# A hand-ordered attention-and-MLP kernel: decay scan and weight decoding as single steps, a new order for all queues, and one pool of PSUM banks

## Chip, core and metric

The kernel runs on one core of a Trainium2 chip. The metric is the device time of one execution in microseconds (us). TensorE (PE) does the matmuls, its weight loads are the row PEld; VectorE is DVE, ScalarE is ACT, GpSimd is POOL, and SP's queue issues the DMA loads and stores.

## What is computed

A gated linear attention, followed by an MLP with a hardswish. The first runs over 4 batches of 8 heads, 768 tokens and 48 columns a head; the second takes its output as 3072 tokens of 384 columns.

```python
for t in range(S):                       # S = 768, for each of 4 x 8 heads
    state = alpha[t][:, None] * state + outer(k[t], v[t])
    y[t] = q[t] @ state
x = y.transpose(0, 2, 1, 3).reshape(3072, 384)
h = x @ w_in                             # 384 x 2048
g = h * clip(h + 3, 0, 6) / 6
out = g @ w_out                          # 2048 x 384
```

The weights come in float64 and are passed as pairs of 32-bit words, so the kernel decodes them itself.

## The kernel before

**Attention.** The 3072 tokens are cut into 24 chunks of 128 (`j` = 0 to 23, six a batch). Per chunk: the decay is scanned backwards over the chunk (`r`, a scan on VectorE, and the reciprocal of its first column), then forwards from that reciprocal (`p`). `k` and `q` are multiplied with the two scans (steps `k`, `q`), scores are formed on TensorE (`sc`) and masked on VectorE (`m`); `qa`, `sv` are ScalarE copies that put q and the state beside the scores and v; `kb`, `ck` turn k by token (for later chunks `kt`, `kw`, `kr` do that by a VectorE transpose and a trip through DRAM); `u` and `sm` update the state, `st` (POOL) decays it; `ya`, `yb` form the output and `cy` copies it out. For the first six chunks alpha, k and q are transposed on TensorE (`ta`, `tk`, `tq`) and alpha is copied by ScalarE (`ca`); from chunk 6 on VectorE transposes them. `la`, `lk`, `lq`, `lv` load alpha, k, q, v.

**Weights.** 16 slices of 768 KB: 0 to 7 are `w_in`, 8 to 15 `w_out`. `w` loads a slice into a staging buffer (five at first, three from slice 5 on). `d1` and `d2` (ScalarE, `dx` for slices 0, 1, 2, 4), `d3` (VectorE, two instructions for these four slices, three for the others), and `d4` (POOL) decode it. A staging buffer is loaded again only after `d4`.

**MLP.** Two chunks form a group. Groups 0 and 1 take the plain first layer: `f` (or by halves `fa`, `fb`), `fr` on ScalarE and `fg` on VectorE make the hidden values. Group 0 takes the plain second layer `b`. From group 2 on the first layer is a scheme of sums and 20 products in which fewer products are needed: `xc` sums the inputs (VectorE), `M` is a product (TensorE, line 600), `n` copies a partial bank to SBUF (ScalarE, line 606) before the next product goes on in the same bank, `o` combines (VectorE), `e` and `h` gate. `y` sums the weights once. From group 1 on the second layer does the same with 7 products `P` (line 703), sums `s`, copies `K`, outputs `G` (VectorE, or ScalarE for the fourth) and stores `O`; `x` sums its weights. `z` are matmuls of the identity that feed nothing.

**What sets the order.** Every step is a word, `name.numbers`; one list of 1788 words is walked under a manual schedule, and each engine's queue holds its instructions in the order of the list. An engine waits for the first instruction of its queue. The last number of many words is a buffer: a PSUM bank for steps that write one (`M.2.0.2`: product 0 of group 2 in bank 2), one of 16 slots for `n` and `s`.

**PSUM.** Eight banks with two lists of names: `banks` (4, line 223) for the attention steps, `bank_m` (4, line 470) for the MLP and `z`.

Lines used below: 186, 191, 196 `d1`, `dx`, `d2`; 199 `high_bits` (`d3`); 217 `d4`; 282 TensorE transposes; 300 `ca`; 309 and 313 the first scan and its reciprocal in `decay`; 320 `p`; 332 `k`, `q`; 346 `sc`; 356 `m`; 378 `ck`; 429 `u`; 439 `sm`; 455 `ya`, `yb`; 478 `f`; 489 `fa`, `fb`; 494 `fr`, `e`; 498 `fg`, `h`; 516 `b`; 532 `z`; 537 to 541 sums; 647 `x`, `s`; 682 `K`; 719 `G`.

Of the kernel before, what the change touches and what calls it, by code (L numbers as in the profile page):

```python
# [9 lines left out]
U32 = mybir.dt.uint32  # L10
# [7 lines left out]
def kernel(  # L18
# [42 lines left out]
    G = 2  # L61
# [116 lines left out]
    def slice_of(i):  # L178
        dst, raw = weight_dst(i), raw_of(i)
        lo, hi = (raw[:, :, x].rearrange("p (m n) -> p m n", m=dst.shape[1]) for x in range(2))  # L180
        return dst, lo, hi
# [17 lines left out]
    def high_bits(i):  # L199
        dst, _, hi = slice_of(i)  # L200
        bits = dst.bitcast(U32)
        if i in BY_HALVES:
            nc.vector.tensor_scalar(dst, dst, 2.0**16 * LOWEST, 2.0**16 * HIGHEST, ALU.max,
                                    ALU.min)
            nc.vector.tensor_single_scalar(bits, bits, 3, op=ALU.logical_shift_left)
        else:
            nc.vector.tensor_scalar(dst, dst, LOWEST, HIGHEST, ALU.max, ALU.min)
            nc.vector.tensor_scalar(bits, bits, 3, 0x3FFFFFF8, ALU.logical_shift_left,
                                    ALU.bitwise_and)
            nc.vector.scalar_tensor_tensor(hi, hi, 0xC0000000, bits, ALU.bitwise_and,  # L210
                                           ALU.bitwise_or)
# [92 lines left out]
    def decay(j):  # L304

        n = NP * W
        ax, ic = aX[j % 2], ini[j % 2]
        R = Rs[j % 2]
        nc.vector.tensor_tensor_scan(  # L309
            out=reverse(R, n - 1, n), data0=reverse(ax, n, n), data1=reverse(ones, n, n),  # L310
            initial=0.0, op0=ALU.mult, op1=ALU.add)
        R_t[j] = R.rearrange("r (p w) -> r p w", w=W)
        nc.vector.reciprocal(out=ic.rearrange("r (p w) -> r p w", w=W)[:, :, 0:1],
                             in_=R_t[j][:, :, 0:1])
# [155 lines left out]
    bank_m = [ps.tile([C, GT * 2], FP, tag=f"m{i}", name=f"m{i}_ps") for i in range(4)]  # L470

# [249 lines left out]
    def store2(g, i):  # L721
# [9 lines left out]
        "d1": round_low, "d2": magnitude, "dx": sign, "d3": high_bits, "d4": add_low,  # L731
        "ta": lambda j, *i: transposed("a", j, *i), "tk": lambda j, *i: transposed("k", j, *i),
        "tq": lambda j, *i: transposed("q", j, *i), "ca": place_alpha, "r": decay, "p": growth,
# [16 lines left out]
    with tc.manual_schedule():  # L750
        run("""z.0.5 z.0.3 z.0.1 z.0.8 qa.0.0 w.0 d2.0 d3.0 la.0 ta.0.0 ca.0 r.0 lk.0 tk.0.1 k.0
               z.0.2 p.0 la.1 ta.1.2 lq.0 tq.0.3 ca.1 r.1 lk.1 lv.0.0 sv.0.0 d1.0 kb.0.0 ck.0 z.0.2
               u.0.2.1 sm.0.0 sv.0.1 q.0 qa.0.1 tk.1.0 k.1 p.1 z.0.2 sc.0.2.3 m.0 la.2 ta.2.0 ca.2
               dx.0 w.2 d2.2 kb.1.0 ck.1 lq.1 r.2 sm.0.1 st.1 tq.1.2 q.1 d3.2 z.0.3 d1.2 dx.2 lv.1.1
               u.1.3.1 sv.1.0 sm.1.0 p.2 sm.1.1 sc.1.0.2 m.1 ya.0.3 yb.0 cy.0 lq.2 w.1 d1.1 tq.2.1
               q.2 d4.2 lk.2 tk.2.3 k.2 fa.2.0 d4.0 st.2 sc.2.0.2 d2.1 d3.1 m.2 dx.1 d4.1 qa.1.1
               lk.3 la.3 ta.3.1 ca.3 la.4 fa.0.1 sv.1.1 w.3 r.3 ta.4.3 ca.4 r.4 tk.3.1 k.3 kb.2.0
               qa.1.0 d2.3 ya.1.2 yb.1 cy.1 fa.1.2 lq.3 ck.2 d1.3 p.3 d3.3 lv.2.2 u.2.3.2 sm.2.0
               d4.3 fb.2 tq.3.1 q.3 fb.1 qa.2.0 sm.2.1 sv.2.0 st.3 fr.0.2.0 fg.0.2 lk.4 tk.4.0
               sv.2.1 w.5 d2.5 k.4 d3.5 d1.5 qa.3.0 d4.5 qa.2.1 sc.3.1.3 m.3 w.6 d2.6 d1.6 d3.6 d4.6  # L760
               lv.3.0 lq.4 w.7 kb.3.2 fb.0 f.0.3.3 kb.4.0 ya.2.1 ck.3 u.3.3.2 sm.3.0 fr.0.3.1 fg.0.3
               fr.0.1.0 fg.0.1 qa.3.1 sv.3.0 sm.3.1 p.4 d2.7 sv.3.1 d1.7 d3.7 d4.7 f.0.5.0 fr.0.5.1
               fr.0.0.0 fg.0.5 fg.0.0 tq.4.3 ck.4 la.5 ta.5.2 f.0.6.3 ca.5 w.4 d2.4 ya.3.0 yb.3 cy.3
               fr.0.6.1 yb.2 cy.2 w.9 d2.9 q.4 qa.4.1 d1.4 d1.9 dx.4 la.6 w.8 d3.4 r.5 lk.5 w.10
               d3.9 p.5 ca.6 fg.0.6 d4.9 w.12 lq.5 lv.4.1 d2.8 d3.8 f.0.7.2 d1.8 st.4 d4.8 d4.4 w.11
               fr.0.7.0 fg.0.7 f.1.7.0 fr.1.7.1 fg.1.7 sc.4.0.2 m.4 f.1.1.1 fr.1.1.0 fg.1.1 f.1.3.3
               fr.1.3.1 d2.10 d1.10 tk.5.3 f.1.0.2 d2.12 d3.10 d4.10 w.13 fg.1.3 fr.1.0.0 fg.1.0 k.5
               d3.12 lq.6 f.1.6.0 f.1.2.1 u.4.1.0 sm.4.0 d1.12 d4.12 sv.4.0 qa.4.0 ya.4.2 fr.1.6.1
               fg.1.6 w.15 tq.5.3 fa.4.3 sv.4.1 d2.11 kb.5.1 d2.13 fr.1.2.0 f.1.4.2 fr.1.4.1 d1.11
               sm.4.1 q.5 r.6 d3.11 d3.13 fg.1.4 d4.11 lv.5.0 lk.6 tq.6 p.6 d2.15 d3.15 fg.1.2 d1.13  # L770
               d4.13 sc.5.0.3 yb.4 f.1.5.0 fr.1.5.1 fg.1.5 tk.6 m.5 b.1.0.2 fb.4 b.1.1 d1.15 d4.15
               st.5 y.5 w.14 la.7 lk.7 cy.4 d2.14 qa.5.1 ck.5 b.0.0.1 fr.0.4.0 d3.14 k.6 q.6 ca.7
               fg.0.4 d1.14 d4.14 x.0 y.1 y.10 b.0.1 y.0 y.2 u.5.2 P.1.0.0 K.1.0 qa.5.0 sv.5.0
               qa.6.1 P.1.1.3 b.0.2 b.1.2 kb.6.0 ya.5.3 y.6 s.1.0.0 sm.5.0 sv.5.1 G.1.0.0 tk.7
               s.1.1.1 s.1.2.3 x.1 yb.5 cy.5 b.1.3 sc.6.1.2 lv.6.2 ck.6 u.6.3.0 s.1.3.2 x.2 P.1.2
               b.0.3 K.1.1 y.7 s.1.4 s.1.5 y.11 y.3 r.7 xc.2.1 x.3 y.4 y.8 xc.2.3 k.7 xc.2.0 xc.2.4
               y.9 y.12 y.16 y.13 y.15 P.1.3.3 K.1.2 P.1.4 bo.1 P.1.5 xc.2.5 G.1.1.1 P.1.6 y.14 y.17
               y.19 xc.2.6 sm.6.0 G.1.2.2 y.20 M.2.0.2 lv.12.1 la.8 O.1.1 O.1.0 ca.8 y.18 y.21 y.23
               so.1 G.1.3.3 n.2.0.8 bo.0 lq.7 lv.7.0 O.1.2 m.6 xc.2.2 xc.2.10 xc.2.7 tq.7 r.8 p.7
               xc.2.8 sv.6.1 M.2.15.3 M.2.1 kb.7.3 n.2.1.9 M.2.16 M.2.2 n.2.2.10 M.2.7.0 n.2.7.11  # L780
               sm.6.1 xc.2.9 q.7 p.8 M.2.3 M.2.4 n.2.4.12 M.2.8 o.2.0.0 M.2.5 n.2.5.13 qa.7.0 sv.6.0
               st.7 lk.8 O.1.3 lq.8 lk.9 la.9 la.10 tk.8 tq.8 lq.10 lq.9 ya.6.1 yb.6 M.2.9 z.1.3
               M.2.18.1 o.2.1.0 e.2.1.1 M.2.10 cy.6 ck.7 sc.7.0.2 u.7.1.3 n.2.10.14 M.2.11 qa.7.1
               ca.9 la.11 y.22 M.2.6.2 h.2.1 q.8 m.7 e.2.0.0 h.2.0 n.2.11.15 qa.6.0 n.2.18.10 qa.8.1
               M.2.12 M.2.19 n.2.12.12 M.2.13 sm.7.0 sv.7.1 r.9 k.8 o.2.3.0 sv.7.0 ya.7.0 y.24
               o.2.5.0 n.2.13.12 o.2.2.0 yb.7 cy.7 sc.8.1.2 xc.3.1 o.2.2.1 e.2.2.1 xc.3.3 o.2.3.1
               M.2.14 xc.3.4 xc.3.0 xc.3.5 o.2.4.0 xc.3.7 xc.3.6 o.2.6.0 P.2.0.1 M.3.0.2 M.2.17
               h.2.2 o.2.6.1 e.2.3.0 h.2.3 o.2.7.0 K.2.0 n.3.0.12 M.3.1 n.3.1.9 e.2.5.1 M.3.7.0
               n.3.7.13 xc.3.8 o.2.7.1 xc.3.2 kt.8 e.2.6.0 h.2.6 tk.9 M.3.2 n.3.2.10 e.2.4.0 P.2.1.3
               h.2.4 h.2.5 s.2.0.14 e.2.7.0 G.2.0.1 h.2.7 M.3.3 M.3.4 n.3.4.8 k.9 s.2.1.11 M.3.8  # L790
               o.3.0.0 ca.10 kt.9 P.2.3.3 s.2.2.15 s.2.3.14 lv.8.2 kw.8 kr.8 lk.10 sm.7.1 xc.3.9
               M.3.5 n.3.5.11 K.2.2 e.3.0.1 xc.3.10 M.3.9 o.3.1.0 P.2.2 K.2.1 u.8.0.3 M.3.18.2 s.2.5
               M.3.10 n.3.10.14 n.3.18.15 e.3.1.0 s.2.4 P.2.4 tq.9 h.3.0 st.8 sv.8.0 M.3.11 n.3.11.8
               tk.10 p.9 sm.8.0 q.9 r.10 k.10 qa.9.0 qa.9.1 m.8 sm.8.1 h.3.1 M.3.19 o.3.5.0 kt.10
               P.2.5 G.2.2.0 st.9 M.3.12 sc.9.0.1 qa.8.0 n.3.12.10 o.3.3.0 kw.9 lv.9.0 kr.9 sv.8.1
               u.9.2.3 sm.9.0 sv.9.1 sv.9.0 G.2.1.2 sm.9.1 st.10 M.3.15.2 M.3.16 M.3.6.3 M.3.13 m.9
               o.3.4.0 o.3.6.0 tq.10 n.3.13.10 o.3.2.0 e.3.4.1 ya.8.2 yb.8 ya.9.3 yb.9 cy.9 M.3.14
               M.3.17 cy.8 xc.4.1 P.2.6 e.3.5.0 G.2.3.3 o.3.2.1 xc.4.3 h.3.4 xc.4.4 o.3.6.1 xc.4.5
               xc.4.0 xc.4.6 e.3.2.1 M.4.0.0 n.4.0.10 P.3.0.1 xc.4.7 o.3.7.0 p.10 h.3.5 o.3.3.1
               xc.4.8 M.4.7.3 M.4.1 xc.4.2 h.3.2 o.3.7.1 lk.11 O.2.2 tk.11 e.3.6.0 e.3.3.1 h.3.3  # L800
               P.3.1.2 e.3.7.1 n.4.1.13 M.4.2 K.3.0 ca.11 q.10 h.3.6 r.11 k.11 h.3.7 n.4.7.15
               lv.10.2 lv.11.0 kw.10 sc.10.0.1 kr.10 G.3.0.0 u.10.3.2 sm.10.0 qa.10.1 n.4.2.14 M.4.3
               M.4.4 M.4.8 s.3.0.9 xc.4.9 s.3.2.12 s.3.1.11 P.3.3.2 n.4.4.8 M.4.5 o.4.0.0 e.4.0.0
               sv.10.1 sm.10.1 xc.4.10 kt.11 O.2.0 O.2.3 lq.11 m.10 s.3.3.9 s.3.5 M.4.9 o.4.1.0
# [128 lines left out]
```

## Time and profile before

| what | value |
|---|---|
| median of three runs | 535.61 us (535.24 to 535.81) |
| profiled execution, first to last instruction | 533.7 us, granted TensorE clock 1.000 |
| PE busy | 524.6 us (98%), 6306 instructions |
| DVE busy | 477.2 us (89%), 849 instructions |
| ACT busy | 257.2 us (48%), 503 instructions |
| POOL busy | 50.4 us (9%) |
| chain that ended last | PE 85%, DVE 8%, POOL 2%, DMA 2%, ACT 1% |

The time of a run is longer than the span of the profiled execution by 1.9 us; the span counts from the first to the last instruction of the core. Matmul durations overlap in the records, so PE's busy time says only when it has work. The first scans and decoding steps fall in the first 95 us, in which the weight slices are loaded; from there to the end the products of lines 600 and 703 fill TensorE.

### The profile page before, as it was taken

To read this page: it belongs to the slowest core of one execution; us is meant where nothing else is said; L and a number is where in the kernel's file an instruction comes from. 1 tells how busy PE (TensorE), PEld (TensorE's weight loads), DVE (VectorE), ACT (ScalarE), POOL (GpSimd) and SP (SyncE) were. 2 spreads that over 40 slices of the span, in tenths; PEclk is the share of its full clock that TensorE was granted. 3 is DMA by queue.
4 is the path that set the end of the run, shared out by engine and by line. 5 is a ranking of instruction groups with operands and counts; after the bars stand their busy time and mean duration, and the time that the engine had idled before them with its cause. 6 is when DMAs were issued, how large, how long until landed. Compare 5 with 4: busy or idle time off the path is not lost.

```text
span 533.7 us, 15143 instructions
## 1 busy us (share of the span) xinstructions
PE 524.6 (98%) x6306; PEld 499.4 (94%) x6306; DVE 477.2 (89%) x849; ACT 257.2 (48%) x503; POOL 50.4 (9%) x71
## 2 busy tenths in 40 slices
PE   8799999999999999999999999999999999999997
PEld 7698886789999999999999999999999999999997
DVE  6999989999999999998999999999999899496382
ACT  3889865212653553553544444642634544553340
POOL 5333425100000000000000000000000000000000
DMA  9998876005615155254344355044454042100001
GB/s 174 217 252 256 215 216 152 21 2 154 152 30 116 32 121 135 57 140 95 87 110 113 91 124 140 19 120 102 115 136 104 11 110 43 44 2 2 15 16 37
DMA packets 124100, 54.40 MB, mean 102 GB/s; under 512 B 83328, under 2 KB 116864, under 8 KB 124032
## 3 DMA queue, kind: packets, MB, share of 16 engines
q1 hardware_dynamic: 124032, 53.44, 42.5%
q8 instruction: 49, 0.80, 0.6%
q14 instruction: 19, 0.16, 0.1%
HBM read 44.50 MB, written 8.91 MB: 100 GB/s over the span
## 4 chain that ended last, share of the span: by engine, by line
PE 85%; DVE 8%; POOL 2%; DMA 2%; ACT 1%; issue 1%; SPq 1%; DVEq 0%; POOLq 0%
PE m_ps L703 34%; PE m_ps L600 34%; PE m_ps L478 5%; PE t_ps L455 4%; PE t_ps L346 2%; PE t_ps L429 2%; PE m_ps L489 2%; PE t_ps L282 1%; DVE rings L647 1%; DMA v<-in_v_dram 1%; DVE raw L537 1%; ACT raw L191 1%; DMA kq<-in_k_dram 1%; DVE g_sb L647 1%; DVE w L537 1%
## 5 line engine op out<-in xcount | busy, mean ns | idle before, releaser
L606 ACT COPY g_sb<-m_ps 128x512 f32<-128x512 f32 x110 | 63.6, 584 | 124.9 <-PE m_ps L600 104.1
L703 PE MATMUL m_ps<-w,g_sb 128*128 128x192 f32 x704 | 121.7, 327 | 0.0
L703 PEld LDWEIGHTS m_ps<-w,g_sb 128*128 128x128 f32 x704 | 113.7, 190 | 0.4
L703 PE MATMUL m_ps<-rings,g_sb 128*128 128x192 f32 x528 | 91.5, 326 | 0.0
L703 PEld LDWEIGHTS m_ps<-rings,g_sb 128*128 128x128 f32 x528 | 85.4, 190 | 0.1
L600 PE MATMUL m_ps<-xc,w 128*128 128x128 f32 x640 | 82.7, 277 | 0.3 <-DVE w L541 0.3
L600 PEld LDWEIGHTS m_ps<-xc,w 128*128 128x128 f32 x640 | 77.5, 192 | 1.5 <-issue 0.5
L494 ACT ACTIVATE r<-g_sb,half 128x512 f32<-128x512 f32 x80 | 56.8, 722 | 32.9 <-DVE g_sb L541 12.1
L498 DVE SCALAR_TENSOR_TENSOR g_sb<-r,g_sb 128x512 f32<-128x512 f32 x80 | 53.6, 682 | 4.6 <-ACT r L494 4.2
L600 PE MATMUL m_ps<-xT,raw 128*128 128x128 f32 x400 | 52.5, 277 | 0.0
L600 PEld LDWEIGHTS m_ps<-xT,raw 128*128 128x128 f32 x400 | 48.6, 192 | 0.6
L409 POOL TENSOR_TENSOR st<-sm,R 128x192 f32<-128x192 f32 x20 | 12.9, 643 | 353.8 <-DVE sm L439 306.7
L647 DVE TENSOR_TENSOR g_sb<-g_sb 128x512 f32<-128x512 f32 (+1 forms) x55 | 42.0, 795 | 0.2
L600 PE MATMUL m_ps<-xT,w 128*128 128x128 f32 x320 | 42.0, 276 | 0.0
L600 PEld LDWEIGHTS m_ps<-xT,w 128*128 128x128 f32 x320 | 39.3, 192 | 0.1
L366 ACT COPY A<-q 48x256 f32<-48x256 f32 x88 | 35.5, 404 | 5.0 <-DVE q L332 3.7
L356 DVE TENSOR_TENSOR A<-t_ps,mask 64x256 f32<-64x256 f32 x96 | 36.0, 414 | 0.4
L478 PE MATMUL m_ps<-xT,w 128*128 128x256 f32 x144 | 32.8, 382 | 0.0
L600 PE MATMUL m_ps<-xc,raw 128*128 128x128 f32 x240 | 31.8, 276 | 0.0
L309 DVE TENSOR_TENSOR_SCAN R<-t,ones 128x516 f32<-128x516 f32 x24 | 29.7, 1236 | 1.1 <-ACT t L300 1.0
L478 PEld LDWEIGHTS m_ps<-xT,w 128*128 128x128 f32 x144 | 26.7, 190 | 3.6
L600 PEld LDWEIGHTS m_ps<-xc,raw 128*128 128x128 f32 x240 | 29.6, 192 | 0.1
(104 smaller groups left out, 731.0 us busy)
## 6 DMA issues: line engine op xcount, KB each, us to landing
raw<-in_moe_w_out_dram SPq DMA_DIRECT2D x8, 768.0 KB, 5.2
raw<-in_moe_w_in_dram SPq DMA_DIRECT2D x6, 768.0 KB, 6.8
v<-in_v_dram SPq DMA_DIRECT2D x48, 96.0 KB, 3.0
out_dram<-oh SPq DMA_DIRECT2D x44, 96.0 KB, 1.7
far<-kq SPq DMA_DIRECT2D x64, 64.0 KB, 2.2
kb<-far SPq DMA_DIRECT2D x64, 64.0 KB, 2.0
aq<-in_alpha_dram SPq DMA_DIRECT2D x36, 96.0 KB, 2.5
qq<-in_q_dram SPq DMA_DIRECT2D x36, 96.0 KB, 2.4
```

Of the source, the lines that this page charges most:

```text
L309: nc.vector.tensor_tensor_scan(out=reverse(R, n - 1, n), data0=reverse(ax, n, n), data1=reverse(ones, n, n), initial=0.0, op0=ALU.mult, op ...
L356: nc.vector.tensor_tensor(out=to[:, a], in0=sc[a][half], in1=mask[half, half].unsqueeze(1).to_broadcast([HB, NP, HB]), op=ALU.mult)
L366: nc.scalar.copy(out=to[:, a], in_=Q_t[j][64 * a : 64 * a + D, :, half])
L409: nc.gpsimd.tensor_tensor(out=st, in0=sm, in1=R_t[j][:, :, 0:1].to_broadcast([C, NP, D]), op=ALU.mult)
L455: nc.tensor.matmul(y_of(j, (i + 1) // 2, p)[:, HB * b : HB * b + HB], vb[:, p, e : e + 32], A_t[j][:, b, 2 * p + a], start=(b == 0 and i = ...
L478: nc.tensor.matmul(h[:, f], w1[:, kk, o : o + C], xT_t[g][:, kk], start=(kk == 0), stop=(kk == KT - 1))
L494: nc.scalar.activation(out=to, in_=h, func=AF.Relu, bias=half, scale=1.0 / 6.0)
L498: nc.vector.scalar_tensor_tensor(out=to, in0=r, scalar=1.0, in1=h, op0=ALU.min, op1=ALU.mult)
L600: nc.tensor.matmul(acc[g][i][:, f * C : (f + 1) * C], spots[w][:, f * C : (f + 1) * C], x_of(g, x), start=(first and f == 0), stop=last, s ...
L606: nc.scalar.copy(out=slots[z], in_=acc[g][i])
L647: nc.vector.tensor_tensor(out=out, in0=in0, in1=in1, op=ALU.subtract)
L703: nc.tensor.matmul(to[g], a, rhs[:, f], start=(first and f == 0), stop=(last and f == HF - 1), skip_group_check=True)
```

## The change

`d3` is cut into three steps, `d3` (clamp), `d5` (shift) and, for twelve slices, `d6` (sign), and the reciprocal leaves `r` for a step `ri`. Each word can now stand anywhere that its data allow. The two bank lists are joined, each beginning with its own four, so bank numbers run to 7 and a step of either kind can use any of the eight. The list of words is replaced by one of 1840: the same steps with other banks and slots, in another order. The `z` words hold 29 fillers in both lists.

```diff
-    def high_bits(i):
-        dst, _, hi = slice_of(i)
-        bits = dst.bitcast(U32)
+    def bounded(i):
+        dst = weight_dst(i)
+        by = 2.0**16 if i in BY_HALVES else 1.0
+        nc.vector.tensor_scalar(dst, dst, by * LOWEST, by * HIGHEST, ALU.max, ALU.min)
+
+    def shifted(i):
+        bits = weight_dst(i).bitcast(U32)
         if i in BY_HALVES:
-            nc.vector.tensor_scalar(dst, dst, 2.0**16 * LOWEST, 2.0**16 * HIGHEST, ALU.max,
-                                    ALU.min)
             nc.vector.tensor_single_scalar(bits, bits, 3, op=ALU.logical_shift_left)
         else:
-            nc.vector.tensor_scalar(dst, dst, LOWEST, HIGHEST, ALU.max, ALU.min)
             nc.vector.tensor_scalar(bits, bits, 3, 0x3FFFFFF8, ALU.logical_shift_left,
                                     ALU.bitwise_and)
-            nc.vector.scalar_tensor_tensor(hi, hi, 0xC0000000, bits, ALU.bitwise_and,
-                                           ALU.bitwise_or)
+
+    def signed(i):
+        dst, _, hi = slice_of(i)
+        nc.vector.scalar_tensor_tensor(hi, hi, 0xC0000000, dst.bitcast(U32), ALU.bitwise_and,
+                                       ALU.bitwise_or)
...
     def decay(j):
...
         R_t[j] = R.rearrange("r (p w) -> r p w", w=W)
+
+    def decay_inverse(j):
+        ic = ini[j % 2]
         nc.vector.reciprocal(out=ic.rearrange("r (p w) -> r p w", w=W)[:, :, 0:1],
                              in_=R_t[j][:, :, 0:1])
...
     bank_m = [ps.tile([C, GT * 2], FP, tag=f"m{i}", name=f"m{i}_ps") for i in range(4)]
+    banks, bank_m = banks + bank_m, bank_m + banks
...
-        run("""z.0.5 z.0.3 z.0.1 z.0.8 qa.0.0 w.0 d2.0 d3.0 la.0 ta.0.0 ca.0 r.0 lk.0 tk.0.1 k.0
-               z.0.2 p.0 la.1 ta.1.2 lq.0 tq.0.3 ca.1 r.1 lk.1 lv.0.0 sv.0.0 d1.0 kb.0.0 ck.0 z.0.2
-               u.0.2.1 sm.0.0 sv.0.1 q.0 qa.0.1 tk.1.0 k.1 p.1 z.0.2 sc.0.2.3 m.0 la.2 ta.2.0 ca.2
-               dx.0 w.2 d2.2 kb.1.0 ck.1 lq.1 r.2 sm.0.1 st.1 tq.1.2 q.1 d3.2 z.0.3 d1.2 dx.2 lv.1.1
-               u.1.3.1 sv.1.0 sm.1.0 p.2 sm.1.1 sc.1.0.2 m.1 ya.0.3 yb.0 cy.0 lq.2 w.1 d1.1 tq.2.1
-               q.2 d4.2 lk.2 tk.2.3 k.2 fa.2.0 d4.0 st.2 sc.2.0.2 d2.1 d3.1 m.2 dx.1 d4.1 qa.1.1
...
+        run("""z.5.1 z.7.5 z.5.2 z.7.2 la.0 ta.0.0 z.7.3 ca.0 r.0 la.1 ri.0 ta.1.7 z.4.8 w.0 ca.1
+               r.1 d2.0 lq.0 tq.0.0 lk.0 d3.0 d1.0 dx.0 p.0 w.2 ri.1 tk.0.3 k.0 kb.0.4 q.0 p.1
+               sc.0.7.3 m.0 qa.0.1 lq.1 tq.1.0 lv.0.0 sv.0.0 ck.0 d5.0 z.1.3 u.0.2.3 d2.2 d3.2 d5.2
+               la.2 d1.2 ya.0.7 ta.2.1 dx.2 d4.2 sm.0.0 sm.0.1 sv.0.1 lk.1 tk.1.5 ca.2 yb.0 lk.2
+               q.1 k.1 cy.0 kb.1.6 ck.1 r.2 sc.1.2.1 qa.1.0 tk.2.7 qa.1.1 m.1 st.1 lv.1.1 u.1.4.0
+               sm.1.0 la.3 sv.1.0 sv.1.1 fa.2.1 k.2 ri.2 qa.0.0 p.2 ta.3.4 ca.3 kb.2.1 lq.2 ck.2
+               w.1 d2.1 r.3 ri.3 d4.0 tq.2.3 q.2 sm.1.1 ya.1.6 yb.1 lk.3 lq.3 fa.0.3 tk.3.2 cy.1
+               p.3 d1.1 dx.1 fb.2 fr.0.2.1 w.3 la.4 lv.2.0 st.2 sv.2.0 w.5 d2.3 d1.3 lv.3.2 k.3
+               d3.1 d5.1 tq.3.1 sc.2.0.2 q.3 kb.3.6 ck.3 m.2 fb.0 ta.4.4 d4.1 sc.3.3.0 d3.3 d5.3
+               la.5 d6.3 qa.3.1 u.2.1.2 sm.2.0 fa.1.2 fb.1 qa.3.0 d4.3 lk.4 m.3 f.0.3.5 sm.2.1 ca.4
...
+               n.11.2.10 n.11.7.12 M.11.8 M.11.3 s.10.0.15 M.11.4 e.10.7.1 G.9.3.3 h.10.7 s.10.1.11
...
+               M.11.17 O.10.1 o.11.7.1 P.10.6 h.11.5 h.11.6 O.10.2 s.11.0.14 s.11.2.8 e.11.7.0
+               P.11.1.6 h.11.7 s.11.1.9 O.9.2 G.10.3.1 s.11.3.11 K.11.0 G.11.0.0 P.11.2 K.11.1
+               s.11.5 s.11.4 O.10.3 P.11.3.2 K.11.2 P.11.4 G.11.1.3 O.11.1 P.11.5 G.11.2.1 P.11.6
+               O.11.2 O.11.0 G.11.3.1 O.11.3""")
```

## The prediction

> **What bounds the kernel now.** I read the table by stage first, then the chain of waits, the groups by line, and last the single records of each queue.
>
> ```profile
> core 0: us, PE busy (x) PEld busy (x) DVE busy (x) ACT busy (x) POOL busy (x), PEclk, DMA share, GB/s
> 0.00:9.00 9.00, 7.54 (x43) 7.54 (x44) 4.68 (x12) 2.50 (x3) 7.12 (x20) 1.00 0.97 176
> 9.00:25.00 16.00, 11.74 (x248) 9.38 (x247) 15.37 (x28) 12.41 (x19) 2.73 (x3) 1.00 1.19 210
> 25.00:45.00 20.00, 19.77 (x342) 17.99 (x343) 19.57 (x32) 18.45 (x34) 7.58 (x6) 1.00 1.08 258
> ...
> 180.00:450.00 270.00, 270.00 (x3520) 265.70 (x3520) 256.63 (x473) 126.98 (x266) 8.74 (x14) 1.00 0.41 97
> 450.00:512.00 62.00, 62.00 (x620) 61.50 (x619) 38.98 (x74) 24.82 (x49) 0.00 (x0) 1.00 0.07 18
> 512.00:533.70 21.70, 18.82 (x118) 18.53 (x116) 10.24 (x17) 3.23 (x7) 0.00 (x0) 1.00 0.10 32
> ```
>
> TensorE (PE) is the bound from 25 us on: it idles 0.5 us between 25 and 512. What can be won lies before 25 us, where it idles 5.7 us and runs most of its fillers, and in not losing anything later. The last 2.9 us are the final copy and store, the same in both kernels. VectorE (DVE) is nearly full too, but from 180 us it has 13 us of slack, and more at the end.
>
> The chain of waits, just ahead of the first matmul group of the MLP (`fa.2`, L489 at 24.90):
>
> ```profile
> 16.83 1.93 ACT raw L191
> 18.76 0.67 ACT w L196
> 19.43 0.47 ACT kb L378
> 19.90 0.84 ACT raw L186
> 20.74 0.02 issue
> 20.76 1.95 ACT raw L191
> 22.71 0.07 issue
> 22.78 2.08 POOL w L217
> 24.86 0.04 issue
> 24.90 1.16 PE m_ps L489 x8
> ```
>
> Two 1.94 us sign steps (`dx.0`, `dx.2`) stand in ScalarE's queue before the slice that `fa.2` needs, then POOL's add. VectorE, timeline at one scan:
>
> ```profile
> 112.44 1.26 DVE L309 TENSOR_TENSOR_SCAN R<-t,ones 128x516 f32<-128x516 f32 x1
> 113.73 0.18 DVE L313 RECIPROCAL t<-R 128x4 f32<-128x4 f32 x1
> 113.83 0.26 DVE L537 TENSOR_TENSOR xc<-xT 128x128 f32<-128x128 f32 x1
> 114.00 1.75 DVE L647 TENSOR_TENSOR rings<-w,rings 128x1536 f32<-128x1536 f32 x1
> ```
>
> An instruction that needs nothing of its neighbour starts about 80 ns before the neighbour ends (113.83 against 113.91). The reciprocal, which reads the scan, starts 34 ns after its end. So a dependent neighbour costs 114 ns; in the records this holds for 64 of the 70 dependent neighbours (the other six wait longer).
> [...]
>
> **Part 1, the split steps.** No instruction is added or dropped: the 52 more words are 16 `d5`, 12 `d6`, 24 `ri`, cut out of `d3` and `r`. I went through both lists and counted VectorE neighbours of which the second reads the first's result. Before: 70 (28 in the decode, 24 scan to reciprocal, 7 `xc`, 11 others). After: 83 (14 decode, 3 scan to reciprocal, 7 reciprocal to second scan, 25 `xc`, 10 `o`, 24 others). So the new order has 13 more, +13 x 0.114 = +1.5 us of VectorE in all, though 2 fewer up to the decode of slice 3 (10 to 8, -0.2 us). All of that hides under TensorE as long as VectorE stays ahead of it.
>
> **Part 2, the banks.** Both name lists now reach all 8 PSUM banks. That adds no instruction; it only removes waits for a bank. The trace shows no TensorE wait of over 0.3 us after 45 us, so I take 0 (a gain of at most the 0.5 us of idle).
>
> **Part 3, the start.** New order of loads: la.0, la.1, w.0, lq.0, lk.0, w.2, lq.1, lv.0, la.2, lk.1, lk.2, lv.1. In the landing events of the trace a 192 KB load lands 1.2 us after the one ahead (6.8, 8.0, 9.2, 10.4, 11.7), a weight slice 2.1 us after (14.0 to 16.1). The first five are the same bytes as before, so lk.0 lands at 10.4, then w.2 12.5, lv.0 14.9, lk.1 17.3, lv.1 19.7. la.0 alone: between 3.5 (1.2 us after the first packet, about 2 us, plus a little) and 5.6 (w.0, four times the bytes, landed first then); I take 4.5.
> - Ten fillers instead of 17 stand before the first transpose: 20 records x 213 ns from 1.5 = 5.8. Transpose 0.7, copy 0.58: the first scan starts at 7.1 (9.3 before, with `d3.0`, 1.5 us, ahead of it). VectorE then runs through: its work up to `k.1` adds to 12.4, so `k.1` ends at 19.8.
> - ScalarE: `d2.0`, `d1.0`, `dx.0` (0.93, 0.93, 1.94) are done while it would wait; `d2.2` follows `qa.0`, `ck.0` at 14.5, then `d1.2`, `dx.2` to 18.3, POOL 2.07: slice 2 at 20.4 (24.86 before).
> - TensorE: `kb.1` after `k.1` 20.3, `ck.1` 20.9, `tk.2`, `u.1` 22.1. So `fa.2` at 22.1 (24.9 before).
> - `f.0.3` needs slice 3. VectorE's work through `d6.3` is 27.0, and 27.0 + 7.7 of start and small waits = 34.7, POOL's 1.47 and 0.1: 36.3. TensorE's own work from `fa.2` to it, 13.5, plus 0.9 of waits, gives 36.5. Before: 40.19.
>
> So `f.0.3` starts 3.7 us earlier; what is late there is slice 3, no longer slice 2. Less of TensorE's work lies behind it: `tk.4` (4 x 109 ns = 0.44) and two fillers (4 records x 112 ns = 0.45; `z.4.3` and `z.5.2` run when nothing is idle). Net -2.8 us. Bounds: 0, if the decode pipeline holds it up again, to -3.7.
>
> **Part 4, the middle.** For each TensorE step I compared the VectorE work queued through its last VectorE producer with the TensorE work queued ahead of it. Before, VectorE needs a lead of up to 2.0 us (`P.2.3` on `s.2.1`); after, at most 0.8 (`P.3.1` on `h.3.3`), and as a product's first half doesn't need that operand, below 0. So VectorE should not stop TensorE. Cover gone: each us that VectorE is late is a us. Weight slices go through three staging buffers: w.12 waits for POOL's `d4.9` and is issued near 63 (59.6 before), and `d2.12` waits for it near 65 to 68; the decode still ends before the steps that read it. On SP's queue `lv.4` now stands behind w.9, which waits for `d4.6` near 49; it lands near 52, and `u.4` reads it near 59. I take 0, with +3 as the upper bound.
>
> **Part 5, the end.** New: `P.11.2` follows one product (2.60) after `P.10.6`, and between them on VectorE stand `h.11.6` (which overwrites what `P.10.6` reads), `s.11.0`, `s.11.2`, `h.11.7`, `s.11.1`, `s.11.3`: 6 x 0.6, four dependent, = 4.2. Its second half (after 1.3) starts late: 4.2 - 3.9 = +0.4 with the handovers. Before, two M groups and a product lie there. Bounds 0 to 1.6.
>
> **Sum**, against the profiled execution's 533.7: -2.8 + 0.4 = 531.3. The median shown, 535.61, is 1.9 above that span; I carry that over: **533.2**.
>
> **Rivals.**
> 1. *Forecast*, 533.2, 531.0 to 534.5: chance 0.55.
> 2. *The lead is given back by 100 us*: the staging buffers or VectorE stall later steps, since the same slices pass the same three buffers at 768 KB each and VectorE was 98% busy from 25 to 45. For: VectorE already idles 2.3 of the 50 us from 45 to 95, in waits. Against: part 4. Then -2.8 + 2.8 to 3 and the end: 535.6 to 536. Chance 0.2. To this belongs that the change doesn't do what it says: +1.5 of dependent neighbours is all that is left, hidden.
> 3. *Slower: the product-copy-product loops.* Between `M.i` and `M.i+1` ScalarE copies the bank (`n`). From a product's last record to its copy is 0.31, the copy 0.58, to the next product 0.05: with one other product (0.89) between there is 0.06 to spare. Before, 7 such loops have 0.9 or less between; after, 27. An `e` (722 ns) in ScalarE's queue at that moment costs up to 0.66. At 0.3 each, 20 more cost 6 us: 533.2 + 6 = 539. It decides from 0.12 per loop on. Against: ScalarE is busy only 127 of 270 us there, and the 7 loops of before show no wait. Chance 0.2.
> 4. *Clock.* Fillers take 213 ns a record up to 6.96 us, 111 after. If la.0 lands after 5.8, TensorE idles and the step may come later: 16 records of `z.4.8` at 213 instead of 111 = 1.6 us late: 534.8. Chance 0.05.
> [...]
>
> **Numbers.** About 0.2% (1.07 us) is what a measurement of this kernel can tell from no change. Faster (below 534.5): 0.55 and little else, 0.57. Same: most of rivals 2 and 4, 0.2. Slower: rival 3 and a bad case of 2, 0.23. Range 531.0 to 537.5: part 3's full gain without part 5, to the lead lost and a few loops missed.
>
> **What would show it.** First scan near 7.1, `fa.2` (first L489) near 22.1, first L478 near 36.5; TensorE without idle from 45 to 510; a gap of under 0.5 us in L703 near the end; VectorE's idle in 180 to 450 smaller than 13 us. Wrong: L478 starts at 39 or later; TensorE waits on ACT at L600 (rival 3); fillers still at 213 ns after 7.5 us (rival 4); waits on DMA in ACT L196 that reach TensorE (rival 2).

## The result and the profile after

The new kernel takes **539.06 us** (median of four runs, 537.86 to 540.64) against 535.42: ratio 1.0070, 95% interval 1.0051 to 1.0089. It is slower by 0.7%, where 533.2 and faster was forecast. The profiled execution took 538.66, its span is 536.9, 3.2 more than the 533.7 of before, at a granted clock of 0.994 instead of 1.000.

The table by stage of the new kernel, with the columns of the one in the prediction. Its lines stand some lines further down than those of the kernel before: 286 transposes, 338 `k` and `q`, 380 `kb`, 435 `u`, 461 `ya` and `yb`, 470 `cy`, 485 `f`, 496 `fa`, 607 `M`, 710 `P`, 726 `G`, 221 `d4`.

```profile
core 0: us, PE busy (x) PEld busy (x) DVE busy (x) ACT busy (x) POOL busy (x), PEclk, DMA share, GB/s
0.00:9.00 9.00, 7.54 (x47) 7.54 (x48) 4.67 (x13) 3.08 (x4) 6.96 (x20) 1.00 0.85 178
9.00:25.00 16.00, 13.70 (x259) 11.77 (x258) 15.28 (x27) 13.78 (x24) 5.05 (x3) 0.89 1.17 212
25.00:45.00 20.00, 19.23 (x424) 17.38 (x423) 19.71 (x35) 18.31 (x33) 8.65 (x6) 1.00 1.03 239
45.00:95.00 50.00, 47.98 (x386) 39.73 (x386) 45.21 (x72) 36.01 (x56) 18.48 (x23) 0.97 0.81 208
...
180.00:450.00 270.00, 268.83 (x3504) 263.87 (x3503) 258.14 (x472) 127.71 (x266) 9.67 (x14) 1.00 0.43 95
450.00:512.00 62.00, 62.00 (x648) 61.40 (x648) 38.97 (x71) 25.24 (x51) 0.00 (x0) 1.00 0.07 18
```

The kernel before had in the stage from 45 to 95:

```profile
45.00:95.00 50.00, 50.00 (x484) 40.36 (x484) 47.70 (x73) 34.72 (x55) 21.66 (x26) 1.00 0.74 197
```

Two columns differ. PE is 2.0 us short of full in 45 to 95, where before had 50.00; and PEclk is below 1 in two stages (0.89 and 0.97). From 45 to 95 VectorE too does 2.5 us less than before (45.21 against 47.70): it stood still as well.

The chain of waits of the new kernel (start, us, what) names the place:

```profile
22.35 1.54 PE m_ps L496 x12
...
36.92 2.59 PE t_ps L485 x12
...
43.21 0.44 PE m_ps L380 x4
43.65 0.58 PE t_ps L461 x30
44.23 2.79 issue
47.02 0.28 PE t_ps L461 x2
47.30 0.73 PE t_ps L485
```

`fa.2` (L496 here) and `f.0.3` (L485) come early, as forecast. Then TensorE stops for 2.79 us after 30 of the 32 records of `yb.3`, and "issue" means that the profile shows nothing that it waited for. TensorE's four waits for another engine in this trace (1.46 us at the first filler, 1.80 at `kb.0`, 0.47 at `kb.1`, 0.76 at `P.6.6`) stand at the first record of a group; between the 30th and the 31st record there is nothing to wait for in the program.

**Where the time went.** I summed, record by record, what the distance between two TensorE records exceeds the usual distance for that pair of shapes, and set both kernels side by side at equal work done. Up to 42 us the new one gains 2.5. The stop in `yb.3` costs 3.0, the records behind it 1.75 (`f.0.5` takes 0.43 instead of 0.22 us a record). From 51 to 275 us it wins 0.9, small waits of the old order that are gone. From 275 to 356 it loses 1.3, of it 0.9 at `P.6.6`; from there on 0.9, of it 0.6 in a second "issue" stop inside `M.9.14` at 435.6. That is +3.5; fewer changes of shape between neighbouring records take off 0.3: +3.2, the difference of the spans. The 3.0, the 0.9 at `P.6.6` and the 0.6 are single gaps; the sums over long stretches depend on what is taken as the usual distance, and each is good to about 0.6 us.

**The clock.** The table of TensorE alone, cut into stretches of 3.41 us that begin where the recorded clock changes (us, PE busy, PEclk, DMA share, GB/s), at the start and around the stop:

```profile
6.20:9.62 3.42, 3.42 (x32) 1.00 1.09 185
9.62:13.03 3.41, 1.58 (x16) 1.00 1.14 297
13.03:16.44 3.41, 3.41 (x46) 0.50 1.51 164
16.44:19.86 3.42, 2.97 (x104) 1.00 1.26 146
```

```profile
40.33:43.74 3.41, 3.41 (x136) 1.00 1.00 320
43.74:47.16 3.42, 0.63 (x32) 1.00 1.09 359
47.16:50.58 3.42, 3.42 (x10) 0.50 1.10 226
```

A stretch in which TensorE was busy 1.58 or 0.63 of 3.41 us is followed by one at half clock; a stretch with 2.97 is not. The first comes from the 1.80 us that `kb.0` waits for `k.0`, the second from the stop. I call such a stretch a window: the recorded changes of the clock, at 6.20, 13.03, 16.44, 47.16 and 50.58 us, are whole multiples of 3413 ns apart (2, 1, 9 and 1), and the window ahead of the first half-speed one was 46% busy. Of the 17 kernels traced here 16 have a record of the clock. In them a stretch at full clock with up to 1.35 us of work was always followed by one at half clock, one with 1.89 us or more never, and of eleven with 1.41 to 1.73 us eight were. One half-clock window is 3.41 x 0.5 / 537 = 0.0032 of clock, so the four runs of the new kernel can be counted: 537.86 at clock 0.997 (one window), 538.66 and 539.45 at 0.994 (two), 540.64 at 0.990 (three).

**What the stop is.** DMA queue q8 moves 49 packets of 16 KB in each execution (the page: `q8 instruction: 49, 0.80`). TensorE's 12,723 records (6306 matmuls, as many weight loads, 111 of its sequencer) come to 260 a packet, and the stops of this kind stand whole multiples of 256 records apart (1473 and 10945 here, the others in experiment 3), so I read a packet as a block of 256 of its instructions: an estimate, by which the records make 49.7 blocks. Counted from 0, packet n begins at the earliest when TensorE has issued 256 n + 150 records or so (151 over all traces). I call that its point. In the new kernel the point of packet 4 was reached at 40.2 us, the packet began at 44.50 and ended at 45.52; TensorE had stopped at 44.01, after 1473 records, and went on at 47.02. The DMA view of 44 to 48 us shows what stood beside it:

```profile
q1 hardware_dynamic: 2118, 1.26, 114.6%
q8 instruction: 1, 0.02, 1.6%
...
raw<-in_moe_w_out_dram SPq DMA_DIRECT2D x1, 768.0 KB
rings<-in_q_dram SPq DMA_DIRECT2D x1, 192.0 KB, 9.2
```

The data queue keeps all 16 engines busy with weight slices and a load of q (the packets' times add to 114.6% of theirs), and the one packet of instructions begins 4.3 us after its point, where it mostly begins 0.5 to 1.5 us after it in the quiet stretches. Meanwhile `ya.2 yb.2 ya.3 yb.3`, four groups of 64 instructions, had been issued within 3 us.

So **theory I**: TensorE's program is supplied by DMA in blocks; a run of short matmuls that issues some 300 instructions faster than a block arrives stops TensorE, and while weights are being loaded a block takes 6 to 7 us. **Theory II** (operand): the stop belongs to what `yb.3` reads. **Theory III**: it is the short matmuls alone, whatever the DMA does.

### The profile page after: what moved, and what is told of

Its sections match the earlier page's. It is cut to its first block, busy times and chain, and to the rows that moved or that the text cites. A ratio compares the mean times of both kernels' runs of the same rounds, so it can differ in the third digit from the quotient of the medians.

```text
span 536.9 us, 15105 instructions
## 1 busy us (share of the span) xinstructions
PE 526.3 (98%) x6306; PEld 501.9 (93%) x6306; DVE 476.0 (89%) x849; ACT 257.9 (48%) x503; POOL 52.6 (10%) x71
## 3 DMA queue, kind: packets, MB, share of 16 engines
HBM read 44.50 MB, written 8.91 MB: 99 GB/s over the span
## 4 chain that ended last, share of the span: by engine, by line
PE 91%; SPq 3%; DVE 2%; DMA 1%; issue 1%; ACT 0%; POOL 0%; DVEq 0%; POOLq 0%
PE m_ps L710 20%; PE m_ps L607 18%; PE t_ps L710 16%; PE t_ps L607 13%; PE t_ps L485 4%; PE m_ps L461 2%; PE m_ps L485 2%; PE t_ps L523 2%; PE m_ps L523 2%; PE t_ps L461 2%; PE m_ps L496 2%; PE t_ps L352 2%; SPq L266 1%; PE m_ps L435 1%; PE t_ps L539 1%
## 5 line engine op out<-in xcount | busy, mean ns | idle before, releaser
L710 PE MATMUL t_ps<-w,g_sb 128*128 128x192 f32 x352 | 61.0, 327 | 0.0
L710 PE MATMUL m_ps<-w,g_sb 128*128 128x192 f32 x352 | 61.0, 327 | 0.0
L710 PEld LDWEIGHTS m_ps<-w,g_sb 128*128 128x128 f32 x352 | 56.9, 190 | 0.4
L710 PEld LDWEIGHTS t_ps<-w,g_sb 128*128 128x128 f32 x352 | 56.8, 190 | 0.1
L710 PE MATMUL m_ps<-rings,g_sb 128*128 128x192 f32 x288 | 50.2, 327 | 0.0
L607 PE MATMUL m_ps<-xc,w 128*128 128x128 f32 x352 | 46.9, 277 | 0.4 <-issue 0.4
L710 PEld LDWEIGHTS m_ps<-rings,g_sb 128*128 128x128 f32 x288 | 46.8, 190 | 0.5
L710 PE MATMUL t_ps<-rings,g_sb 128*128 128x192 f32 x240 | 41.6, 327 | 0.8 <-DVE oh L726 0.8
L710 PEld LDWEIGHTS t_ps<-rings,g_sb 128*128 128x128 f32 x240 | 38.7, 190 | 0.9 <-DVE oh L726 0.9
L607 PE MATMUL t_ps<-xc,w 128*128 128x128 f32 x288 | 38.0, 276 | 0.0
```

The source lines that it names most:

```text
L607: nc.tensor.matmul(acc[g][i][:, f * C : (f + 1) * C], spots[w][:, f * C : (f + 1) * C], x_of(g, x), start=(first and f == 0), stop=last, s ...
L710: nc.tensor.matmul(to[g], a, rhs[:, f], start=(first and f == 0), stop=(last and f == HF - 1), skip_group_check=True)
```

## Experiments

Medians in us; each ratio is to the kernel before, whose median was 535.41 to 535.50 beside them. Where kernels of different sets are compared, I compare their ratios.

**1. `f.0.5` ahead of `yb.3`** (`f05_first`).

```diff
-kb.4.7 sm.3.1 yb.3 w.7 d2.6 r.5 f.0.5.7 p.4
+kb.4.7 sm.3.1 f.0.5.7 yb.3 w.7 d2.6 r.5 p.4
```

> One word of the new order is moved: `f.0.5` (12 records of 0.22 us) runs ahead of `yb.3` instead of behind it. Theory I (instruction supply): TensorE's program comes in blocks of 256 instructions over the DMA engines; from the point where a block is asked for, TensorE holds some 300 instructions, and four 32-record groups (256 instructions) eat them in 2 us, while that fetch took 4.3 us to begin. With `f.0.5` (24 instructions in 2.7 us) in the middle of them the block lands in time: the 3.0 us stall inside `yb.3` goes, and with it the half-speed window of the clock that followed it (1.7 us); `f.1.2` may wait about 0.5 us for `cy.3`. 539.06 - 4.7 + 0.5 = 534.8. Theory II (operand): the stall belongs to what `yb.3` reads, and goes with `yb.3`; 538 to 539, with a stall of up to 3 us inside `yb.3` at its new place, or less by the 2.7 us it starts later.

Measured 534.58, ratio 0.9983 (0.9974 to 0.9992). TensorE's timeline at the place (start, us, line, records):

```profile
42.42 0.60 PE L380 MATMUL m_ps<-ident,k 128*128 128x128 f32 x4
42.86 2.75 PE L485 MATMUL t_ps<-xT,w 128*128 128x256 f32 x12
45.55 0.65 PE L461 MATMUL t_ps<-A,v 128*32 128x64 f32 x32
46.81 1.56 PE L485 MATMUL t_ps<-xT,w 128*128 128x256 f32 x6 [0.61 <-ACT xT L470]
```

All 32 records of `yb.3` run in one piece; the 0.61 wait for `cy.3` is the one expected. One word moved takes 4.7 us off by the ratios, and the order is now 0.9 us ahead of the kernel before. Theory II has no stop to show.

**2. Loads later, TensorE's order untouched** (`loads_later`).

```diff
-w.7 ... w.4 ... lk.5 ... lq.5 ... w.8
+w.7 ... w.8 w.4 ... lk.5 ... lq.5
```

> Nothing is moved on TensorE. On SP's queue the load `w.8`, which must wait for a staging buffer until about 42.8 us, goes ahead of `w.4`, `lk.5` and `lq.5`, so that these three (768 + 192 + 192 KB) are no longer queued on the DMA engines when TensorE asks for its block at about 40.2 us. Theory I: the fetch that began at 44.50 begins by 42.5, and the stall inside `yb.3` shrinks from 3.0 to between 0 and 0.8 us; no half-speed window at 47 us, or a shorter effect. 534.5 to 535.5, unless `d2.4` now waits for `w.4` (needed at 53.0). Theory II: 538 to 539, stall unchanged, since neither the order on TensorE nor `yb.3`'s operands change. Theory III (the burst alone starves TensorE, whatever the DMA does): stall unchanged.

Measured 535.00, ratio 0.9993 (0.9976 to 1.0011). The packet begins at 42.59 instead of 44.50, and TensorE's timeline has

```profile
44.30 0.65 PE L461 MATMUL t_ps<-A,v 128*32 128x64 f32 x30
45.11 0.27 PE L461 MATMUL t_ps<-A,v 128*32 128x64 f32 x2 [0.15 <-issue]
```

The stop is still after record 30, but 0.15 instead of 2.79 us long. Same matmuls, same operands, other traffic: theories II and III fall. It isn't a full cure: one of eleven runs took 539.62 at clock 0.993.

**3. A filler in the early gap** (`gap_filled`): `z.3.7` behind `tk.0.3`.

> The new order with one more filler, `z.3.7` (14 records, 28 instructions), in TensorE's idle 1.8 us between `tk.0` and `kb.0` (10.5 to 12.3 us). Clock: the window from 9.6 to 13.0 us is then busy, so the half-speed window from 13.0 to 16.4 goes. I expect its price to be small, since VectorE and the slice-2 chain set the pace there: 0 to -0.5 us; if it had cost in full, -1.7. Theory I on the stall: 28 more instructions ahead of it, so the point where TensorE runs dry moves 14 matmuls forward in the program: between records 15 and 20 of `yb.3` instead of after record 31; its length stays 2.7 to 3.3. Theory II: the stall stays after record 31. Time 538.0 to 539.0 by theory I.

Measured 538.50, ratio 1.0053 (1.0040 to 1.0065).

```profile
43.80 0.49 PE L461 MATMUL t_ps<-A,v 128*32 128x64 f32 x17
47.18 0.43 PE L461 MATMUL t_ps<-A,v 128*32 128x64 f32 x15 [2.89 <-issue]
```

With 14 matmul records more ahead of it the stop comes after record 17 of `yb.3` instead of 30, within the range named (15 to 20), and again after 1473 records of TensorE (weight loads and the sequencer's counted). The second stop moves alike, from behind the 5th record of `M.9.14` to behind the 23rd of 32 in `u.22` ahead of it, 14 records, and grows from 0.42 to 1.28 us. In all traces the stops of this kind come after 449, 705, 1473, 1729, 2753 or 10945 records, always 193 more than a multiple of 256. The early half-speed window is gone (PEclk 1.00 from 9 to 25). What it is worth isn't shown: the ratios of the two kernels differ by 0.9 us with intervals that overlap, and the longer second stop is in that.

**4. Both edits** (`both`).

> The moved `f.0.5` and the filler together. By theory I no half-speed window is left (granted clock 0.999 to 1.000), and runs agree more closely than the 537.9 to 540.6 of the new order: 534.3 to 534.8, so level with or up to 0.2% ahead of the kernel before (535.42). By theory II 538 to 539 with a clock of 0.997.

Measured 534.91, 0.1 above the range given, ratio 0.9988 (0.9979 to 0.9997); all eleven runs at clock 1.000, within 534.28 to 535.37. Its trace still has two stops of the kind, 0.59 us after record 449 and 1.13 us after record 10945.

**5. The stop made in the kernel before** (`dense_extra`), **and the same work spread out** (`spread_extra`).

```diff
+"zz": lambda m, n: [nc.tensor.matmul(bank_m[m][32*(i%4) : 32*(i%4)+32, 0:64],
+     ident[:, 32*(i%4) : 32*(i%4)+32], ident[:, 0:64], start=True, stop=True) for i in range(n)]
-ya.3.0 yb.3 cy.3 fr.0.6.1 yb.2 cy.2
+ya.3.0 yb.3 cy.3 fr.0.6.1 yb.2 zz.1.16 zz.1.16 zz.1.16 zz.1.16 cy.2
```

> The kernel before, with extra work of no use on TensorE: four groups of 16 short matmuls (32 records and 64 instructions each, as many as one attention group), all four right behind `ya.3 yb.3 yb.2` near 52.3 us. Nothing else is changed, and the new order plays no part. By work alone each group costs about 0.5 us (an attention group of the same shape takes that), four of them 1.9: 537.3. By theory I seven groups in a row are 448 instructions in about 3.5 us; the block that is asked for at about 51.4 us begins 3.5 us later in the trace of before, lands after 1.4 and is usable 1.2 to 1.5 after that, and only some 300 instructions are held from the request on: TensorE runs dry for 2.5 to 4.5 us in the middle of the extra groups or in the f group behind them, the profile calls that wait issue, and a half-speed window of 1.7 may follow: 540 to 543.5.

> The kernel before with the same four extra groups, one each behind `f.0.7` (55 us), `f.1.0` (67), `kb.5` (75.5) and `b.0.0` (91). By theory I none of them makes a dense run of 300 instructions, so only the work is paid: 537 to 538 (1.5 to 2.5 over 535.42), no wait called issue of over 0.3 us, no half-speed window. By the rival that what costs is the number of instructions or of short matmuls, the same time as with the four together, within 0.5.

Four groups together: 543.45, ratio 1.0148 (1.0135 to 1.0161). The same four apart: 538.32, 0.3 above the range given, 1.0051 (1.0037 to 1.0066). The work costs 2.9; standing together costs 5.1 more. TensorE in the dense one (L742 is `zz`):

```profile
52.33 1.56 PE L742 MATMUL m_ps<-ident 128*32 128x64 f32 x97
57.98 1.08 PE L742 MATMUL m_ps<-ident 128*32 128x64 f32 x31 [4.09 <-issue]
```

4.1 of the 5.1 is the stop; the rest fits the half-speed window behind it (its clock is 0.997). The spread one has no wait called issue behind 25 us.

**6. The dense run where the DMA engines are quiet** (`dense_calm`): six `zz` groups behind `yb.5` at 106 us.

> The kernel before with six of the same useless groups of short matmuls behind `yb.5` at 106 us, where the DMA engines are busy 1 per cent of the time instead of over 100 per cent. By work alone six cost 6/4 of the 2.86 us that four spread ones cost, so 4.3 at most, 2.9 by the records: 538.3 to 539.8. By theory I the block asked for at about 106 us begins after 1.2, takes 1.1 and is usable 1.3 later, 3.5 in all, while the 300 instructions held last some 2.3: TensorE runs dry for 0.8 to 1.8 us only, against 4.1 where the loads stood ahead of the fetch, and no half-speed window follows: 539 to 541. If the load on the DMA engines made no difference, the wait would be 3 us or more and a half-speed window would follow: 543.

Measured 539.21, ratio 1.0066 (1.0053 to 1.0079).

```profile
105.89 2.17 PE L742 MATMUL m_ps<-ident 128*32 128x64 f32 x139
109.15 0.98 PE L742 MATMUL m_ps<-ident 128*32 128x64 f32 x53 [1.09 <-issue]
```

A longer run, a quarter of the stop: the packet begins 1.1 us after its point and takes 1.1, and TensorE goes on 1.3 after its end (1.4 to 1.5 in the other traces). So a block takes 3.5 us from its point when the engines are idle, and 6 to 7 behind weight slices (6.4 in `dense_extra`, 6.8 in the new kernel, 7.0 in `gap_filled`).

**7. What the split is worth.** `rejoined` puts each reciprocal behind its scan and each `d5` behind its `d3`, with the edit of `f05_first` kept; `d5_early` does it for `d5.0` and, other than its expectation says, for `d5.5` too; `rejoined_late`, `rejoined_36_60` and `rejoined_60_on` for the stretches in their names.

```diff
-r.1 d2.0 lq.0 tq.0.0 lk.0 d3.0 d1.0 dx.0 p.0 w.2 ri.1 ... ck.0 d5.0
+r.1 ri.1 d2.0 lq.0 tq.0.0 lk.0 d3.0 d5.0 d1.0 dx.0 p.0 w.2 ... ck.0
```

> The new order with `f.0.5` ahead of `yb.3` (so without the stall), and the split steps put back together: each reciprocal right behind its scan, each `d5` right behind its `d3`. By my count dependent VectorE neighbours rise from 83 to 103, 20 x 0.114 = +2.3 us of VectorE. By my part 1 that hides under TensorE except ahead of slice 3: 0 to +0.7, so 534.6 to 535.3 against 534.58 with the split order. If keeping dependent instructions apart were what the new order lives from: +2.3 or more, 536.9.

> `f.0.5` ahead of `yb.3` as before, and of the split steps a single one put back: `d5.0` (0.69 us on VectorE) right behind `d3.0`, which is ahead of `p.0` and `k.0` instead of behind `m.0`. Dependent neighbours: 84 against 83. Theory P (the split pays by what VectorE does first at the start, not by spacing): `k.0` and with it `kb.0` come 0.6 to 0.8 us later, the idle gap of TensorE ahead of `kb.0` grows from about 1.7 to about 2.5, and a half-speed window is more frequent: 535.2 to 537.0, so a third to two thirds of what `rejoined` lost (3.2). Theory S (spacing of dependent instructions everywhere): 534.6, no change.

> `f.0.5` ahead of `yb.3`, and all the split steps behind `f.0.3` (36 us on) put back together, those at the start left as the new order has them. Dependent neighbours: 101 against 83, +18 x 0.114 = +2.1 us of VectorE, nearly as many as in `rejoined`. Theory P: hidden under TensorE: 534.3 to 535.2, as `f05_first` (534.58). Theory S: nearly all of the loss of `rejoined`, 536.5 to 537.5.

> `f.0.5` ahead of `yb.3`; only the six split steps between `f.0.3` and `f.1.7` (36 to 60 us) put back together: `d5.5`, `ri.4`, `d5.6`, `ri.5`, `d5.7`, `d5.4`. Dependent neighbours 88 against 83: +0.6 us of VectorE by the count. Theory D (the decode of slice 7 is the only place behind 25 us where VectorE sets TensorE's pace): most of the 1.85 us is here: 535.6 to 536.4. Theory S (spacing everywhere): 534.58 + 1.85 x 5/18 = 535.1.

> `f.0.5` ahead of `yb.3`; only the 21 split steps behind `f.1.7` (60 us on) put back together. Dependent neighbours 94 against 83, +1.3 us of VectorE. Theory D: hidden, 534.2 to 535.0. Theory S: 534.58 + 1.85 x 11/18 = 535.7.

| kernel | dependent neighbours | us | ratio (95%) |
|---|---|---|---|
| `f05_first` | 83 | 534.58 | 0.9983 (0.9974 to 0.9992) |
| `rejoined` | 103 | 537.76 | 1.0039 (1.0025 to 1.0054) |
| `d5_early` | 84 | 535.83 | 1.0005 (0.9996 to 1.0014) |
| `rejoined_late` | 101 | 536.43 | 1.0010 (1.0002 to 1.0019) |
| `rejoined_36_60` | 88 | 535.63 | 1.0005 (0.9997 to 1.0014) |
| `rejoined_60_on` | 94 | 534.95 | 0.9991 (0.9982 to 1.0000) |

`rejoined` missed my 534.6 to 535.3 by far, and `rejoined_late` missed 534.3 to 535.2. By ratios `d5_early` costs 1.2 us, the six steps between 36 and 60 us 1.2 (`d5.5` is one of them), and the 21 steps behind 60 us 0.4, whose interval overlaps that of `f05_first`; each of these differences is good to about 0.7. `rejoined` has 3.0 and `rejoined_late` 1.4; the first moves `ri.0`, `ri.1`, `ri.2` too, both move `d5.8` and `d5.9` too, and no part tries these. The cost does not go with the number of dependent neighbours (+1, +5, +11). It goes with what stands behind them. No run moves `d5.0` alone; but in the trace of `d5_early` TensorE has no wait of over 0.15 us between 26 and 48 us, and `d5.5` runs at 41, so its loss is laid to `d5.0`. That step ahead of `k.0` lengthens TensorE's wait ahead of `kb.0`, here in `d5_early`, where `f05_first` has 1.4 as the longest and all nine kernels whose lists begin with the same words 1.2 to 1.9:

```profile
PE m_ps L380 <- DVE k L338: 2.6, 2, 2.4
```

and the clock of 9 to 25 us falls to 0.79 (this execution is the slowest of its twelve). Between 36 and 60 the decoding of slice 7 is the last thing that TensorE needs of VectorE; `rejoined_36_60` waits there for POOL's `d4.7`, which `f05_first` does not, and that is 0.7 of its 1.2:

```profile
PE t_ps L485 <- POOL w L221: 0.7, 1, 0.7
```

A part of the differences is not the edits'. With the same words up to 36 us, 4 of 11 runs of `f05_first`, 7 of 12 of `rejoined_36_60` and 10 of 11 of `rejoined_60_on` have a clock below 0.999, so at least one half-speed window; of `d5_early` it is 11 of 12. So the 0.4 behind 60 us is no sign of a cost of spacing.

**8. All visible losses mended** (`best`, `best2`, `best3`).

```diff
-kw.18 ... O.5.1                            -cy.21 ... u.22.1.2 ... M.9.14
+O.5.1 kw.18                                +cy.21 M.9.14 ... u.22.1.2
-yb.3 ... w.4 cy.3 f.1.2.6 ... lk.5 tk.5.5
+yb.3 ... w.4 lk.5 tk.5.5 cy.3 f.1.2.6      (best2 also: fa.0.3 between ya.1.6 and yb.1)
```

> Every loss that the trace of the new order shows, mended by moving words: `f.0.5` ahead of `yb.3`; `tk.5` and `tq.5` between `yb.3` and `f.1.2`, over the 0.68 us wait for `cy.3`; the store `O.5.1` ahead of the load `kw.18` on SP's queue, so that `G.6.1` and with it `P.6.6` no longer wait for that store (0.5 to 0.9 us); `M.9.14` ahead of `ya.20`, into the middle of five short groups that ran TensorE dry for 0.3 to 0.6 us. 534.58 - 0.5 - 0.7 - 0.4 = 533.0, ratio to before 0.9955 (0.9945 to 0.997).

> The mended form of the kernel that took its words from everywhere: `f.0.5` ahead of `yb.3`; `lk.5` directly behind `w.4` and `tk.5` ahead of `f.1.2`, over the wait for `cy.3`; `O.5.1` ahead of `kw.18`; `M.9.14` ahead of `ya.20`; and `fa.0` between `ya.1` and `yb.1`, where two traces showed a wait called issue of 0.4 to 0.8 us. Every word reads what it read. 534.58 - 0.4 - 0.5 to 0.9 - 0.3 - 0 to 0.4: 533.0 to 533.6.

> `f.0.5` ahead of `yb.3`, `lk.5` behind `w.4` and `tk.5` ahead of `f.1.2`, `O.5.1` ahead of `kw.18`, `M.9.14` ahead of `ya.20`; `fa.0` left in its place. In the traces the mended places held 0.68 + 0.48 + 0.28 us of waits, of which `tk.5` covers 0.5: 534.58 - 0.5 - 0.5 - 0.3 = 533.3, 533.0 to 534.4.

`best` (without the moved `lk.5`, with `tq.5` moved too) took 534.38, ratio 0.9978 (0.9969 to 0.9987), but its `tk.5` runs ahead of the load it should read and its `tq.5` writes a bank that `fr.0.3` and `fg.0.3` still read, so chunk 5 and part of group 0's hidden values are other values. The two that keep every value gave 534.84 (0.9985, 0.9977 to 0.9994) and 534.49 (0.9986, 0.9977 to 0.9995): no better than `f05_first`. `best2` is 1.2 us above its range; `best3` is 0.1 above its range and 1.2 above the 533.3 that I added up; `best` missed its 533.0 too. In the trace of `best3` the wait was only passed on: `tk.5` waits 1.5 us for its load, in place of `f.1.2`'s 0.61 for `cy.3`. The waits at `P.6.6` and `M.9.14` (0.48 and 0.28 us in `f05_first`) are gone in all three, but that is less than the executions of one kernel differ (533.7 to 535.9). None with the right values beats the one word moved, which is 0.17% ahead of the kernel before.

## Why the prediction was wrong

- **The bound and where a gain can lie**: right. TensorE is the bound, and what the new order wins it wins ahead of 25 us.
- **Part 1** (+13 dependent neighbours, +1.5 us of VectorE, hidden): the count holds (83), 624 other neighbours overlap, and TensorE waits for no VectorE result in 45 to 340 us. VectorE idles 11.9 us in 180 to 450 (under 13, as forecast). But the question was put too narrowly: I priced the gaps and not the freedom to move a step. Experiment 7 puts that at about 3 us, most of it at two places where VectorE does set the pace, the start and, argued from one wait of 0.7 us, the decoding of slice 7.
- **Part 2** (banks, 0): no run tried it alone; no TensorE wait of the new kernel is for a bank except `P.6.6`, below.
- **Part 3** (start): first scan at 7.30 (7.1 forecast), `fa.2` at 22.29 (22.1), `f.0.3` at 36.76 (36.5); slice 2 ready at 19.9 (20.4). Net -2.5 (-2.8).
- **Part 4** (middle, "I take 0, with +3 as the upper bound") is **the step that failed**: it measured +4.75 at 44 to 50 us, 3.0 for the stop in `yb.3` and 1.75 for the half-speed window behind it. Its check was whether VectorE's, POOL's and SP's work is ready in time, and up to 340 us it was. It never asked whether TensorE's own instructions are. The four short groups in a row, the weight slices on the DMA engines and the 4.0 us that a packet of q8 took to begin in that stretch of the kernel before (from 33.6 to 37.6 us) were all to be had from the list of words and the old trace.
- **Part 5** (end, +0.4): no wait over 0.06 us at `P.11.2`; 0.
- **Not seen**: `P.6.6` (+0.9). The store `O.5.1` now stands behind `kw.18` and `kr.18` on SP's queue, so `G.6.1` waits for its buffer and `P.6.6` for the bank:

```profile
353.62 0.36 DVE L726 TENSOR_TENSOR oh<-t_ps,p 128x192 f32<-128x192 f32 x1 [1.53 <-DMA out_dram<-oh]
...
354.03 2.87 PE L710 MATMUL t_ps<-rings,g_sb 128*128 128x192 f32 x16 [0.76 <-DVE oh L726]
```

- **The sum** would have been too good without the stop as well: `f05_first` is 0.9 us ahead of the kernel before, where the forecast had 2.2 to 2.4 (533.2 against 535.42 or 535.61). In its trace TensorE is about 2.9 us ahead at 50 us and 0.8 at the end; the waits in between are 0.6 for `cy.3`, 0.7 for a weight slice at 100 us, 0.5 at `P.6.6` and 0.3 in `M.9.14`.
- **Rivals.** Rival 2 had the course (the lead given back by 100 us) with the wrong cause: no staging buffer and no VectorE wait. Rival 3 came out at the very time, 539, and is false: behind 100 us TensorE waits nowhere for ScalarE; with 27 tight product loops none cost anything. A time that fits is no proof of a mechanism.
- **Rival 4** looked for the clock at the wrong place. la.0 came in time: TensorE's first records stand 213 ns apart, from 6.2 us on about 111 (from 7.0 before). But the wait ahead of `kb.0` and the stop each brought a half-speed window.

## What to carry to other kernels

Before a list of instructions is reordered, count TensorE's instructions, not only its time: in these traces a block of 256 took 3.5 us to arrive with the DMA engines idle and 6 to 7 behind large loads, against some 300 instructions in hand, so four or five short-matmul groups in a row want a long-matmul group in between. A wait that the profile calls "issue", in the middle of a group and at a fixed number of instructions modulo 256 (193 in these traces), was that stop; 14 matmuls more ahead of it moved it from behind the 30th to behind the 17th record of `yb.3`. Then look at the clock: here a window of 3.41 us with up to 1.35 us of work cost the next one half its speed, and one with 1.89 or more did not.

## What was not expected of the hardware

The page lists the instruction supply among the DMA queues (q8, 49 packets, 0.80 MB), and its packets began later where the engines that move the data were busy. Over all packets of the 17 traces, one of q8 began 1.0 us after its point (median; 0.6 to 1.5 in eight of ten) where the engines were under 10% busy in the 2 us behind the point, and 3.0 after it (2.0 to 4.3) where they were over 90% busy. At the three long stops, with slices of 768 KB under way, it was 3.6 (`dense_extra`), 4.3 (the new kernel) and 4.5 (`gap_filled`). TensorE stopped 299 records after a block's point (1473 against the 1174 of packet 4 in the new kernel), and a stop cost 0.15 (`loads_later`) to 4.1 us (`dense_extra`) where short matmuls stood together. Why a packet begins late behind queued data, and what passes in the 1.3 to 1.5 us between its end and the next matmul, no run here takes apart.
